# Softmax attention, soft mixture of experts and a gated layer: inverse roots from Ln and Exp, attention in double steps

## The chip, the core and the metric

The kernel runs on one core of one Trainium2 chip. The metric is device time in microseconds (us), the median of several executions. Five engines work side by side, each through its own instructions in order: TensorE (PE in the profile, with its weight loads as PEld), VectorE (DVE), ScalarE (ACT), GpSimd (POOL) and SyncE (SP), which here only issues DMA transfers.

## What is computed

Three layers follow one another: attention over 4 batches x 12 heads (448 tokens, 64 columns a head), a soft mixture of experts, and a gated layer. The part that the change touches is the first:

```python
def rmsnorm(x, g):
    rms = np.sqrt(np.mean(x * x, axis=-1, keepdims=True) + 1e-06)
    return x / rms * g
q_n, k_n = (rmsnorm(q, g_q), rmsnorm(k, g_k))
scale = 1.0 / np.sqrt(q.shape[-1])
scores = scale * np.matmul(q_n, k_n.transpose(0, 1, 3, 2))
scores = scores - np.max(scores, axis=-1, keepdims=True)
attn = np.exp(scores)
attn = attn / (np.sum(attn, axis=-1, keepdims=True) + 1e-09)
return np.matmul(attn, v).astype(np.float32)
```

Its output is the `x` of `_moe_ref` (logits, two softmaxes, 8 experts with relu), and that one's output is the input of `(x @ w_a) * (x @ w_b) @ w_out`.

## The kernel before

**Attention.** Heads are worked on in 24 pairs. The loop `for j in range(NPAIR + 1)` (L597) has one turn for a pair, and eight steps `s8` in it; a step is one block of 112 query rows of one head, numbered `n = 8 * j + s8`. What a step issues on each engine stands in the order of the code, since PE, ACT, POOL and SP follow the order of the program in this part; only DVE's order is chosen by a scheduler when the kernel is built.

A block goes through these functions. `score(n)` (L346) makes 112 x 448 scores with two matmuls (L357, L358; tile `pss`, one bank of PSUM, pool `ps_s` with three) and DVE searches the row maxima (L359, `nmx`). `expo(n)` (L363) takes the exponential on ACT (L368, tile `p`) and sums it. `ptrans(n)` (L374) transposes `p` with four PE instructions (L381, tile `pspt`, pool `ps_p` with two banks) and copies the result to `pt` on ACT (L387), or on DVE (L385) in two of eight steps. `av` (L389) multiplies the transposed probabilities of the pair before with `v` (L395, tile `psv`). In the loop, step n issues `score(n + 2)`, `expo(n + 1)`, in odd steps `av`, and `ptrans(n)`.

**The queries and keys to come.** The pairs ahead are made ready in the same loop. POOL squares (`square`, L252, tile `sq`, two buffers), DVE sums (`sumsq`, L260), and `rsqrt(p)` (L271) computes the inverse root on DVE alone: a bit trick gives a first guess, and three Newton steps follow, 12 small instructions of 112 x 16 elements in all (L281 to L291), which `tick` spreads between other work. `normalise(p)` (L294) multiplies on POOL. `emit_T(p, 0)` and `emit_T(p, 1)` (L310) transpose queries and keys (L324, tile `pst`), ACT writes a rounded part to the tile `e` (L326, L329) and DVE the rest (L327, L330). `e` has one buffer. `emit_Z(p)` (L335) then issues six DMA transfers on SP (L342 to L344, three for each head) that rearrange `e` into the tiles `z` which `score` reads; there are four, two for a pair. So the ACT write to `e` for the next pair waits until all six transfers of this pair have landed. In turn j, `emit_T(j + 2, 0)` stands in step 4, `emit_T(j + 2, 1)` in step 5, `emit_Z(j + 2)` in step 6, and the first `score` that reads these tiles in step 6 of turn j + 1.

**Other work in the loop.** `bcast` (L417; tile `psbc`, ACT copy `rd` L426) and `finish` (L429) divide the attention output. From turn 7 on, parts of the mixture of experts' first stage (`moe_tasks`, L443) are put in, one `task()` in each of the steps 3, 6 and 7. `pst`, `psbc` and the tasks take PSUM banks from the pool `ps_m` (two).

**Prologue.** Before the loop, pairs 0 to 3 are prepared (L555 to L589) and the first scores issued; `warm` issues matmuls that compute nothing needed.

**After attention.** The experts run on weights that SP streams from memory (L136), into seven places that take over attention's memory and a ring of five; then the gated layer. Neither is edited.

## Time and profile before

| | us |
|---|---|
| median of 3 runs | 597.33 (596.6 to 600.82) |
| profiled execution | 597.8, of which the span from first to last instruction is 596.0 |
| attention loop, first `score` to last `finish` | about 19.5 to 349.6 |
| busy: PE, DVE, ACT, POOL | 561.1, 388.2, 354.5, 116.5 |
| mean granted TensorE clock | 0.990 |

Busy time is what the profile gives each instruction from start to end; PE's instructions overlap in it. The chain of waits is a better guide to what sets the end: it is followed back from the last instruction, at each point to whatever was waited for, and gives each piece only the time that it adds. "issue" in it is a short hand-over.

### The profile page before, as it was taken

How to read it: one execution, taken by the hardware profiler on the slowest of the kernel's cores; microseconds unless marked ns; L12 is line 12 of the kernel's file. 1: busy time of each engine (PE TensorE's matmuls, PEld its weight loads, DVE VectorE, ACT ScalarE, POOL GpSimd, SP SyncE). 2: the span in 40 equal slices, each digit the busy share in tenths (PEclk: the TensorE clock that was granted, in tenths of full speed). 3: DMA queues.
4: the chain of work that ended last, by engine and by line, in shares of the span. 5: the costliest groups of instructions: out<-in, count | busy, mean ns of one | idle time of the engine just before them, and what ended most of it. 6: DMA issues, size and time to landing. Idle time of an engine off the chain costs nothing.

```text
span 596.0 us, 11201 instructions
## 1 busy us (share of the span) xinstructions
PE 561.1 (94%) x4008; PEld 369.1 (62%) x4008; DVE 388.2 (65%) x919; ACT 354.5 (59%) x797; POOL 116.5 (20%) x135
## 2 busy tenths in 40 slices
PE   6889899999999999999999998898999999999997
PEld 6655555555655565655656545443585656589996
DVE  6888898888899888898776621122227988742210
ACT  4667777778787777877778721111168989542210
POOL 2234343333343343333110000010100000300000
PEclk9999999999999999999999999989999999999999
DMA  5965677786777978696766789999999994002332
GB/s 145 224 164 139 158 175 173 208 230 196 190 221 170 251 177 244 146 268 167 219 184 154 273 343 340 426 408 423 425 425 419 382 398 186 1 27 80 87 95 84
DMA packets 39575, 134.52 MB, mean 226 GB/s; under 512 B 5856, under 2 KB 25312, under 8 KB 33120
## 3 DMA queue, kind: packets, MB, share of 16 engines
q1 hardware_dynamic: 39520, 133.81, 71.2%
q8 instruction: 32, 0.52, 0.4%
q14 instruction: 23, 0.19, 0.1%
HBM read 95.26 MB, written 5.51 MB: 169 GB/s over the span
## 4 chain that ended last, share of the span: by engine, by line
PE 65%; DVE 11%; DMA 10%; ACT 6%; SPq 5%; issue 3%; POOL 0%; ACTq 0%; DVEq 0%
PE psv L395 9%; PE pspt L381 9%; DMA z<-e 7%; PE pss L357 4%; PE pss L358 4%; PE psM L936 4%; PE psh L695 4%; PE pso L1136 3%; PE psS L719 3%; PE pso L1137 3%; PE pso L1138 3%; SPq L343 2%; PE pst L324 2%; DVE nmx L359 2%; PE psL L183 2%
## 5 line engine op out<-in xcount | busy, mean ns | idle before, releaser
L368 ACT ACTIVATE p<-pss,nmx 112x448 f32<-112x448 f32 x192 | 123.4, 643 | 26.0 <-DVE nmx L359 13.5
L359 DVE TENSOR_REDUCE nmx<-pss 112x1 f32<-112x448 f32 x192 | 117.7, 617 | 19.7 <-PE pss L358 18.2
L381 PEld LDWEIGHTS pspt<-ident,p 112*112 112x112 f32 x768 | 80.4, 133 | 78.1 <-ACT pt L387 32.4
L381 PE MATMUL pspt<-ident,p 112*112 112x112 f32 x768 | 110.0, 266 | 1.1 <-ACT p L368 0.9
L395 PE MATMUL psv<-pt,v 112*64 112x448 f32 x368 | 90.3, 569 | 1.0 <-DVE xT L436 1.0
L387 ACT COPY pt<-pspt 112x448 f32<-112x448 f32 x144 | 76.8, 533 | 21.4 <-PE pspt L381 20.5
L357 PE MATMUL pss<-z 128*112 128x448 f32 x192 | 85.2, 444 | 1.7 <-DMA z<-e 1.6
L300 POOL TENSOR_TENSOR n<-xw,rinv 112x512 f32<-112x512 f32 x46 | 48.1, 1066 | 173.6 <-PE pst L324 140.1
L358 PE MATMUL pss<-z 128*112 128x448 f32 x192 | 70.5, 367 | 0.0
L252 POOL TENSOR_TENSOR sq<-xw 112x512 f32<-112x512 f32 x40 | 40.9, 1041 | 0.6 <-DMA xw<-in_q_dram 0.4
L1155 DVE COPY ot<-pso 128x384 f32<-128x384 f32 (+1 forms) x14 | 7.6, 543 | 49.5 <-PE pso L1140 49.5
L357 PEld LDWEIGHTS pss<-z 128*112 128x112 f32 x192 | 34.0, 177 | 9.0 <-issue 7.4
L368 ACT ACTIVATION_READ_ACCUMULATOR p<-pss,nmx 112x1 f32 x192 | 39.4, 205 | 0.0
L816 DVE SCALAR_TENSOR_TENSOR xw<-wu_w,top 128x768 int32<-128x768 int32 x24 | 22.3, 956 | 25.5 <-ACT top L802 25.5
L1136 PE MATMUL pso<-Mh,t 128*128 128x384 f32 x112 | 37.9, 338 | 0.5 <-DVE Ml L965 0.5
L1137 PE MATMUL pso<-Ml,t 128*128 128x384 f32 x112 | 37.7, 337 | 0.0
L1138 PE MATMUL pso<-Mh,t 128*128 128x384 f32 x112 | 37.7, 337 | 0.0
L324 PE MATMUL pst<-ident,n 112*128 112x112 f32 x192 | 27.4, 268 | 10.6 <-ACT rd L426 7.1
L395 PEld LDWEIGHTS psv<-pt,v 112*64 112x64 f32 x368 | 18.3, 135 | 30.7 <-issue 22.5
L385 DVE COPY pt<-pspt 112x448 f32<-112x448 f32 x48 | 29.7, 619 | 10.4 <-PE pspt L381 9.5
L358 PEld LDWEIGHTS pss<-z 128*112 128x112 f32 x192 | 34.2, 178 | 0.7 <-issue 0.6
L260 DVE TENSOR_REDUCE ssq<-sq 112x8 f32<-112x512 f32 x48 | 32.1, 675 | 2.8 <-ACT sq L250 2.6
(177 smaller groups left out, 938.1 us busy)
## 6 DMA issues: line engine op xcount, KB each, us to landing
wu_w<-in_moe_w_dram SPq DMA_DIRECT2D x38, 1536.0 KB, 10.8
z<-e SPq DMA_DIRECT2D x48, 336.0 KB, 4.6
z<-e SPq DMA_DIRECT2D x48, 224.0 KB, 4.4
r<-in_moe_w_dram SPq DMA_DIRECT2D x7, 1536.0 KB, 8.3
xw<-in_moe_w_dram SPq DMA_DIRECT2D x4, 1536.0 KB, 13.4
xw<-in_q_dram SPq DMA_DIRECT2D x24, 224.0 KB, 4.3
xw<-in_k_dram SPq DMA_DIRECT2D x24, 224.0 KB, 4.1
z<-e SPq DMA_DIRECT2D x48, 112.0 KB, 4.4
```

The costliest lines, as they stand in the source:

```text
L252: pool.tensor_tensor(out=sq, in0=a, in1=a, op=ALU.mult)
L300: (eng if eng and i == 0 else pool).tensor_tensor(out=n_t[p][:, i].rearrange("p c h d -> p h c d"), in0=qk_t[p][:, i].rearrange("p h (c d) ...
L357: pe.matmul(ps, x, z[:, 1, :], start=True, stop=False)
L358: pe.matmul(ps, x, z[:, 2, :], start=False, stop=True)
L359: dve.tensor_reduce(out=nm_of[n // 8][:, h % 2, c:c + 1], in_=ps, axis=AX.X, op=ALU.max, negate=True)
L368: act.activation(out=t, in_=ps_of.pop(n), func=AF.Exp, bias=nm_of[n // 8][:, h % 2, c:c + 1], accum_out=den_t[n // 8][:, h % 2, c:c + 1],)
L381: pe.transpose(ps[:, kc * P:(kc + 1) * P], src[:, kc * P:(kc + 1) * P], ident[0:P, 0:P])
L387: act.copy(out=o, in_=i)
L395: pe.matmul(av_t[p][hd * D:(hd + 1) * D, 0:S], v_t[p][hd][:, kc, :], pt_t[2 * p + hd][:, kc, :], start=(kc == 0), stop=(kc == NC - 1),)
L1136: pe.matmul(o, ch[:, m], Mh[:, m, c], start=(m == 0), stop=False)
L1137: pe.matmul(o, ch[:, m], Ml[:, m, c], start=False, stop=False)
L1138: pe.matmul(o, cl[:, m], Mh[:, m, c], start=False, stop=False)
```

## The change

Three things change together.

1. `rsqrt(p)` takes its first guess from ACT: `Ln` of the sum of squares and `Exp` of minus half of that, and one Newton step of three DVE instructions follows. It is called in step 0 of turn j for pair j + 3, instead of step 7 for pair j + 4. A table of ACT's functions is loaded by hand at the start.
2. The eight steps of a turn become four double steps `s4`. `score(n)` now makes two blocks of scores in a tile of two banks, and one DVE search gives both maxima. A double step issues `expo(n + 2)`, `ptrans(n)`, `expo(n + 3)`, `ptrans(n + 1)`, then `score(n + 4)` (both blocks), then `av`. `emit_T(j + 2, 0)` stands at the end of `s4 == 2`, `emit_T(j + 2, 1)` and `emit_Z(j + 2)` at the end of `s4 == 3`, with two tasks behind them.
3. Buffers: `ps_s` has two tiles of two banks, `ps_p` is gone and its tiles come from `ps_m`, which has three banks; `p` has three buffers, `sq` one.

```diff
-        sqp = c1.enter_context(tc.tile_pool(name="sqp", bufs=2))
+        sqp = c1.enter_context(tc.tile_pool(name="sqp", bufs=1))
-        pp = c1.enter_context(tc.tile_pool(name="pp", bufs=2))
+        pp = c1.enter_context(tc.tile_pool(name="pp", bufs=3))
-        ps_s = c1.enter_context(tc.tile_pool(name="ps_s", bufs=3, space=PSUM))
-        ps_p = c1.enter_context(tc.tile_pool(name="ps_p", bufs=2, space=PSUM))
+        ps_s = c1.enter_context(tc.tile_pool(name="ps_s", bufs=2, space=PSUM))
-        ps_m = c1.enter_context(tc.tile_pool(name="ps_m", bufs=2, space=PSUM))
+        ps_m = c1.enter_context(tc.tile_pool(name="ps_m", bufs=3, space=PSUM))
...
-            mf = ssq_t.pop(p).rearrange("p a c -> p (a c)")
...
-            for _ in range(3):
-                small.append((p, lambda: dve.tensor_tensor(out=t, in0=yf, in1=yf, op=ALU.mult)))
...
+            x = ssq_t.pop(p).rearrange("p a c -> p (a c)")
+            act.activation(out=t, in_=x, func=AF.Ln, bias=ssq_eps[0:P])
+            act.activation(out=yf, in_=t, func=AF.Exp, scale=-0.5)
+            small.append((p, lambda: dve.scalar_tensor_tensor(
+                out=t, in0=yf, scalar=-0.5, in1=yf, op0=ALU.mult, op1=ALU.mult)))
+            small.append((p, lambda: dve.scalar_tensor_tensor(
+                out=t, in0=x, scalar=D * 1e-6, in1=t, op0=ALU.add, op1=ALU.mult)))
+            small.append((p, lambda: dve.scalar_tensor_tensor(
+                out=yf, in0=t, scalar=1.5, in1=yf, op0=ALU.add, op1=ALU.mult)))
...
+            ps = ps_s.tile([128, 2, 512], F32, tag="s", name="pss")[0:P, :, 0:S]
+            for i in range(2):
+                x = z[:, 0, (c + i) * P:(c + i + 1) * P]
+                pe.matmul(ps[:, i], x, z[:, 1, :], start=True, stop=False)
+                pe.matmul(ps[:, i], x, z[:, 2, :], start=False, stop=True)
+                ps_of[n + i] = ps[:, i]
+            dve.tensor_reduce(out=nm_of[n // 8][:, h % 2, c:c + 2], in_=ps, axis=AX.X, op=ALU.max, negate=True)
...
-            ps = ps_p.tile([P, 512], F32, tag="pt", name="pspt")[:, 0:S]
+            ps = ps_m.tile([128, 512], F32, tag="m", name="pspt")[0:P, 0:S]
...
+                for i in range(2):
+                    expo(n + 2 + i)
+                    if live:
+                        ptrans(n + i)
+                score(n + 4)
+                av(j - 1, s4)
+                if s4 == 0:
+                    if j > 0:
+                        rsqrt(j + 3)
+                    spread(j - 1)
+                    square(j + 4, 0)
+                elif s4 == 1:
+                    sumsq(j + 4, 0)
+                    square(j + 4, 1)
+                elif s4 == 2:
+                    bcast(j - 1)
+                    normalise(j + 3)
+                    emit_T(j + 2, 0)
+                    if j == 0:
+                        emit_T(j + 2, 1)
+                        emit_Z(j + 2)
+                else:
+                    if j > 0:
+                        emit_T(j + 2, 1)
+                        emit_Z(j + 2)
+                    load_v(j + 1)
+                    sumsq(j + 4, 1)
+                for _ in range(1 + (s4 == 3)):
+                    if s4 in (1, 3) or (s4 == 0 and j > NPAIR - HP):
+                        task()
```

How the rows of the programs move is shown at three places. The first is PE in the second half of turn 1, before: `psbc` and the transposes `pst` stand between single scores, and the second group of `pst` (the keys of pair 3) is followed by five more groups before the turn ends.

```order
L381 MATMUL pspt<-ident,p_549 112x112 x4
L324 MATMUL pst<-ident,n_415 128x112 x4
L422 MATMUL psbc<-ident,bc 128x112 x4
L357 MATMUL pss<-z_142 112x448
L358 MATMUL pss<-z_142 112x448
L395 MATMUL psv<-pt_355,v_177 64x448
L395 MATMUL psv<-pt_408,v_177 64x448
L381 MATMUL pspt<-ident,p_565 112x112 x4
L324 MATMUL pst<-ident,n_415 128x112 x4
L357 MATMUL pss<-z_139 112x448
L358 MATMUL pss<-z_139 112x448
L381 MATMUL pspt<-ident,p_596 112x112 x4
```

The same place after the change, from `psbc` to the second group of `pst`:

```order
L422 MATMUL psbc<-ident,bc 128x112 x4
L323 MATMUL pst<-ident,n_402 128x112 x4
L381 MATMUL pspt<-ident,p_521 112x112 x4
L381 MATMUL pspt<-ident,p_530 112x112 x4
L357 MATMUL pss<-z_138 112x448
L358 MATMUL pss<-z_138 112x448
L357 MATMUL pss<-z_138 112x448
L358 MATMUL pss<-z_138 112x448
L395 MATMUL psv<-pt_355,v_177 64x448
L395 MATMUL psv<-pt_408,v_177 64x448
L323 MATMUL pst<-ident,n_402 128x112 x4
L381 MATMUL pspt<-ident,p_566 112x112 x4
```

What moved: the two groups of `pst` are now a whole double step apart, the second is the last thing of the turn, and the next pair's tile (`z_138`) is already read at this point of turn 1, where before it was read after the second `pst`.

The second place is ACT between the two writes to `e` (`L326` and `L329` before, `L325` and `L328` after), before (turn 2):

```order
L326 ACTIVATE e_574<-pst 128x448
L426 COPY rd<-psbc 128x448
L368 ACTIVATE p_596,den<-pss,nmx 112x448
L329 ACTIVATE e_574<-pst,few 128x448
L368 ACTIVATE p_621,den<-pss,nmx 112x448
```

and after (turn 2):

```order
L426 COPY rd<-psbc 128x448
L325 ACTIVATE e_715<-pst 128x448
L368 ACTIVATE p_723,den<-pss,nmx 112x448
L387 COPY pt_680<-pspt 112x4x112
L368 ACTIVATE p_731,den<-pss,nmx 112x448
L387 COPY pt_680<-pspt 112x4x112
L328 ACTIVATE e_715<-pst,few 128x448
```

What moved: two exponentials and two copies now lie between the two writes, where one copy and one exponential lay before.

The third place is DVE at the end of the prologue, at the first search for maxima (L359 before, L360 after). Before:

```order
L281 TENSOR_SCALAR ssq_316<-ssq_316 112x16
L288 TENSOR_TENSOR nt<-rinv_297 112x16
L283 TENSOR_SCALAR rinv_321<-ssq_316 112x16
L289 SCALAR_TENSOR_TENSOR nt<-nt,ssq_255 112x16
L285 TENSOR_SCALAR rinv_321<-rinv_321 112x16
L359 TENSOR_REDUCE nmx<-pss 112x1
L291 SCALAR_TENSOR_TENSOR rinv_297<-nt,rinv_297 112x16
L288 TENSOR_TENSOR nt<-rinv_321 112x16
L359 TENSOR_REDUCE nmx<-pss 112x1 x2
```

and after (`rinv_282` and `rinv_299` are the roots of pairs 2 and 3, as `rinv_297` and `rinv_321` before):

```order
L329 SCALAR_TENSOR_TENSOR e_245<-pst,few,e_245 128x448
L286 SCALAR_TENSOR_TENSOR nt<-rinv_282 112x16
L288 SCALAR_TENSOR_TENSOR nt<-ssq_240,nt 112x16
L261 TENSOR_REDUCE ssq_294<-sq 112x8
L290 SCALAR_TENSOR_TENSOR rinv_282<-nt,rinv_282 112x16
L261 TENSOR_REDUCE ssq_294<-sq 112x8
L286 SCALAR_TENSOR_TENSOR nt<-rinv_299 112x16
L288 SCALAR_TENSOR_TENSOR nt<-ssq_294,nt 112x16
L290 SCALAR_TENSOR_TENSOR rinv_299<-nt,rinv_299 112x16
L360 TENSOR_REDUCE nmx<-pss 112x2
```

What moved: the first search stood in the middle of the Newton steps of pairs 2 and 3, and now stands behind all of them.

## Rows read from the trace of the kernel before

**Rows 1.** Windows: length, busy us (instructions) by engine, granted clock, DMA share, GB/s

```profile
119.00:313.80 194.80, 188.88 (x1244) 114.90 (x1245) 166.08 (x422) 147.76 (x386) 61.27 (x66) 1.00 0.78 206
...
349.00:490.00 141.00, 130.15 (x1264) 77.96 (x1265) 58.56 (x111) 60.41 (x83) 7.57 (x15) 0.99 0.98 400
```

**Rows 2.** Chain of waits near 210 us: start, us added, engine, tile, line

```profile
209.48 0.53 PE pspt L381 x4
210.01 0.20 PE pss L357
...
210.42 0.38 PE pspt L381 x4
...
211.21 0.90 PE psv L395 x4
...
213.77 0.38 PE pst L324 x4
```

**Rows 3.** Chain of waits, 89 to 106 us: SP's issues and the landing

```profile
89.83 3.97 DMA z<-e
...
97.36 0.47 SPq L342
...
98.52 1.07 SPq L344
...
101.40 4.42 DMA z<-e
```

**Rows 4.** Timeline of ACT: the copy `rd`, one in each turn, turns 1, 7, 21

```profile
42.58 0.53 ACT L426 COPY rd<-psbc 128x448 f32<-128x448 f32 x1
...
118.97 0.55 ACT L426 COPY rd<-psbc 128x448 f32<-128x448 f32 x1
...
313.81 0.56 ACT L426 COPY rd<-psbc 128x448 f32<-128x448 f32 x1
```

**Rows 5.** Timeline of the prologue: start, us, engine, line, operation

```profile
7.70 0.15 DVE L561 SCALAR_TENSOR_TENSOR few<-few 128x1 f32<-128x1 f32 x1
...
15.17 0.63 ACT L329 ACTIVATE e<-pst,few 128x448 fp32r<-128x448 f32 x1 [0.20 <-PE pst L324]
...
20.86 0.63 ACT L368 ACTIVATE p<-pss,nmx 112x448 f32<-112x448 f32 x1 [4.02 <-DVE nmx L359]
```

**Rows 6.** Chain of waits, 24 to 60 us

```profile
33.54 0.43 ACT pt L387
...
34.01 0.73 ACT p L368 x2
...
45.49 1.69 PE psv L395 x4
...
50.03 0.54 PE pspt L381 x4
```

**Rows 7.** Groups by line: busy us, mean ns of one, idle before

```profile
L359 DVE TENSOR_REDUCE nmx<-pss 112x1 f32<-112x448 f32 x192 | 117.7, 617 | 19.7 <-PE pss L358 18.2
L330 DVE SCALAR_TENSOR_TENSOR e<-pst,few,e 128x448 fp32r<-128x448 f32 x24 | 16.1, 671 | 0.1
L326 ACT ACTIVATE e<-pst 128x448 fp32r<-128x448 f32 x24 | 13.2, 550 | 20.9 <-DMA z<-e 13.9 <-PE pst L324 4.9 <-PE pss L358 2.0
L474 ACT ACTIVATE nm<-nm 128x1 f32<-128x1 f32 x2 | 0.6, 294 | 3.5 <-DVE nm L473 3.5
L100 ACT ACT_TABLE_LOAD x1 | 1.3, 1283 | 0.7 <-PEq L1204 0.7
```

**Rows 8.** Timeline near 204 us: POOL's multiplication and two Newton instructions

```profile
201.13 0.17 DVE L289 SCALAR_TENSOR_TENSOR nt<-nt,ssq 112x16 f32<-112x16 f32 x1
...
204.06 2.04 POOL L300 TENSOR_TENSOR n<-xw,rinv 112x512 f32<-112x512 f32 x2 [7.72 <-PE pst L324]
204.11 1.01 DVE L289 SCALAR_TENSOR_TENSOR nt<-nt,ssq 112x16 f32<-112x16 f32 x1
```

**Rows 9.** Chain of waits, 110 to 140 us: a late landing

```profile
127.84 5.77 DMA z<-e
```

87 lines of the change are left out of this document (26 added, 61 removed).

## The prediction

> **What bounds the kernel now.** I read the windows first. In the stretch of attention from turn 7 on, PE is busy 188.9 of 194.8 us; behind attention the DMA engines are busy 98% of the time [rows 1]. So the later stages follow attention's end and move with it as a block; the question is what attention does. The chain of waits tells it: near 210 us it is PE alone. Two steps cost 0.53 us (first group of `pspt`, behind `psv`) + 0.38 (second group) + 4 x 0.205 (scores) + 0.90 (`av`) = 2.63 us [rows 2]. Four of these and three groups of transposes (two `pst`, one `psbc`) at 0.38 make 11.7 us a turn as PE's own floor. The copies `rd` mark the turns: from turn 1 to 7 six turns take 76.4 us, 12.73 each, and from 7 to 21 fourteen take 194.8, 13.92 each [rows 4]. In the first stretch nearly nothing but the 11.7 is to be done, so 1.0 us a turn is stall. In the second, the tasks add PE work: 188.9 / 14 = 13.5 a turn bounds the floor from above, since the busy times of PE overlap a little; I take 13.35, so about 0.55 a turn is stall.
>
> The stall of the first stretch is a loop that the chain shows whole: the six transfers have landed at 89.83 + 3.97 = 93.80, ACT writes `e`, PE transposes the keys, DVE writes its part, SP issues six times, and the next six have landed at 101.40 + 4.42 = 105.82 [rows 3]: 12.02 us, against PE's 11.7. A late landing (5.77 us [rows 9] for 4.42) adds 1.35.
>
> **The change part by part.** *PE's work* is the same: the groups are reordered, and the dear first `pspt` behind `psv` still comes once in a double step. 11.7 stays.
>
> *Fewer DVE instructions.* Nine Newton instructions and three before them go, three stay; two searches become one. DVE is not on the chain where PE is, so this pays nothing by itself; it only lets DVE's part of `e` come sooner. The size: a Newton instruction takes 0.17 us alone and 1.01 when POOL's 2.04 us multiplication runs [rows 8]. One search takes 0.617 [rows 7]; a search of two blocks is not in the trace, and lies between 0.62 (nothing for the second) and 1.23 (no saving); I take 1.1, nearest to twice the row. It hides either way: its exponentials come a double step later.
>
> The row of 1.01 us fits a rule of the Trainium skill (SBUF, section Who interferes with whom): a DVE instruction with two SBUF inputs and a GpSimd instruction that reads SBUF use one read interface, and the second to start waits for the whole of the other. By the rule the three new instructions, which have two such inputs, still wait behind POOL, up to 2 us a turn; by the row alone I would charge 0.8 each time. In the new order they stand behind DVE's part of `e`, so neither enters the sum.
>
> *Ln and Exp.* Not in the trace; the nearest ACT instructions on few columns take 0.294 us [rows 7]. I take 0.3 each, 0 to 0.6 as bounds for both when they overlap others. ACT then has 8 x 0.73 + 6 x 0.43 [rows 6] + 0.55 [rows 7] + 0.63 [rows 5] + 0.45 + 0.6 = 10.7 us a turn, under PE's 11.7: hidden, but only 1 us is left.
>
> *The z loop.* This is the term that speaks against the change. Between ACT's two writes to `e` there were one copy and one exponential; now there are two exponentials and two copies: 2 x (0.73 + 0.43) = 2.32 us. The loop becomes 0.55 (`e`, queries) + 2.32 + 0.63 (`e`, keys) + 0.67 (DVE's part [rows 7]) + 101.40 - 97.36 = 4.04 (first to sixth issue) + 4.42 (landing) [rows 3] + some 0.1 of hand-over = 12.75. That is 0.7 longer than 12.02. Against it stands a DVE that is less late. So a turn without tasks takes 12.75 at best; with one landing in five late by 1.35, 13.0.
>
> *When scores read z.* Before, a whole turn lay between the issue and the first score; now `emit_Z` is last in a turn and `score` of that tile stands in `s4 == 2` of the next. From the last `pst` to that score PE has 2 x 2.63 + 0.91 = 6.2 us of work. The first head's tile needs 0.63 + 0.67 + (98.52 - 97.36 = 1.16, third issue) + 4.42 + 0.1 = 7.0. PE waits 0.8 in a turn without tasks; this lies inside the 12.75 to 13.0 (11.7 + 0.8 = 12.5). With tasks, 1 us and more of their work stands behind the last `pst`, and the wait is covered.
>
> *Three banks for everything.* Behind the last `pst` come two tasks, then `pspt`: the third in turn gets the bank of `pst`, which DVE frees 0.63 + 0.67 = 1.3 us after PE's end. Two `psx` tasks last 0.7, so PE loses 0 to 0.6 in the eleven or so turns with tasks. I take 0.3 on average, 0.2 over fourteen turns.
>
> *Prologue.* Roots of pair 0: DVE waits for `gg` until 7.70 [rows 5]; then three instructions of 0.17 instead of the rest of two Newton chains, so `e` and the first transfers come about 1.6 us sooner. But ACT now issues Ln of pair 2 behind its second write to `e` of pair 1 (15.17 + 0.63 [rows 5], some 0.8 later by my count, so 16.6), and behind that follow in series, with one `sq` buffer: two pairs of Ln and Exp (1.2), two squares (1.25), two sums (1.35), Newton (0.5): 21.0, then the first search. The first exponential starts at 22.1 instead of 20.86 [rows 5]. From there to the end of turn 1 ACT has 18 exponentials, 12 copies, two pairs of writes to `e`, one `rd`, Ln and Exp: 13.1 + 5.2 + 2.4 + 0.5 + 0.6 = 21.8 us; nothing in that stretch waits longer for `z`, since pair 2's roots no longer wait behind searches. So turn 1 ends at about 44.7, with 0.8 us of scores done ahead of where they stood. Before, it ended at 50.03 + 0.54 = 50.57, having waited and then run `psv` at 1.69 us where it takes 0.90 [rows 6, 2]. Gain 5.9 + 0.8 = 6.7, between 2 and 8.
>
> **Sum**, against the profiled 597.8: prologue -6.7; turns 1 to 7: 6 x (13.0 - 12.73) = +1.6; turns 7 to 21: 12 turns with tasks at PE's floor, two without at 13.0 instead of 11.7 (+2.6), the banks (+2.8): 14 x 13.35 + 2.6 + 2.8 = 192.3 instead of 194.8, -2.5; the rest 0. That is -7.6: 590.2, rounded to 590.0. The median of the runs shown is 597.33, 0.5 below the profiled one.
>
> **Rivals.**
> *All stalls go* (chance 0.16). If a DVE that is less busy lets `e` come early and landings are quick, PE sets every turn: -6.7 - 6 x 1.0 - 14 x 0.55 = -20.4: 577. For it: the chain near 210 us is PE alone. Against: the loop of 12.75 is longer than 11.7.
> *The z loop sets every turn* (0.14). If landings take 5.77 as a rule, or ACT reaches the second write to `e` one exponential late, the loop is 14.1 to 14.2 in both stretches: 6 x 1.45 + 14 x 0.25 - 6.7 = +5.5: 603. From 14.2 on, it ends over 1% slower. For it: issue and first use are 5 us closer together. Against: 4.42 is the commoner landing.
> *The gain is given back* (0.23). The prologue gains 3 only, and the banks cost the full 0.6 in eleven turns, so that turns 7 to 21 take 186.9 + 2.6 + 6.6 = 196.1: -3 + 1.6 + 1.3 = about 598.
> *Table loads* (0.02). If Ln and Exp did not sit in one loaded table with the rest, two loads of 1.283 us [rows 7] a turn would put ACT at 13.3 against 11.7: 20 x 1.3 = +26, 617. The new program has one load in all, as before. The Trainium skill (ScalarE: Activation LUTs, section Table sets: the hidden batching unit) says that one set holds both; no run here has shown it yet.
>
> **How the numbers follow.** The forecast has 0.45, with 585 to 595 as its own range. About 1% is what a measurement of this kernel can tell from no change: faster is under 591.4, slower over 603.3. Faster: three quarters of 0.45, all of 0.16 and a little of the third rival, 0.52. Slower: most of 0.14 and the 0.02, 0.14. The rest, 0.34, is within 1%. The range from 577 to 603 leaves out half of the first rival, half of the second and the last.
>
> **What would show it.** Right: `rd` in turn 1 at about 41 instead of 42.58, turns of 12.7 to 13.2 up to turn 7, the six landings still in the chain there, small waits of `pss` for `z`, and one table load. Wrong: turns over 13.5 in the first stretch (the loop was underrated), turns at 11.7 (it was overrated), a first exponential before 20 or after 24 us, PE's clock under full speed in the loop, or a later stage that changes its length.

## The result and the profile after

The changed kernel takes **603.63 us** (median of 4 runs, 601.82 to 608.16) against 597.81 for the kernel before, run beside it (4 runs): ratio **1.0105**, 95% interval 1.0071 to 1.014. It is slower by 1%, where 590.0 was forecast, and 603 was the upper end of the range. The profiled execution took 601.82 us, its span 600.0, against 597.8 and 596.0 before.

First three windows of the changed kernel, cut at its `rd` of turns 1, 7 and 21 and where the experts' transfers set the pace (columns as in [rows 1]), then these three `rd` in the timeline of ACT.

```profile
45.60:125.00 79.40, 73.50 (x471) 44.65 (x470) 57.74 (x95) 59.22 (x164) 27.82 (x30) 1.00 0.65 156
125.00:322.40 197.40, 189.48 (x1244) 116.33 (x1242) 142.58 (x259) 148.32 (x411) 60.96 (x66) 1.00 0.76 205
...
356.00:494.00 138.00, 127.75 (x1264) 77.29 (x1263) 57.75 (x110) 60.44 (x83) 7.58 (x15) 1.00 1.00 416
```

```profile
45.62 0.53 ACT L426 COPY rd<-psbc 128x448 f32<-128x448 f32 x1 [0.89 <-PE psbc L422]
...
124.95 0.53 ACT L426 COPY rd<-psbc 128x448 f32<-128x448 f32 x1 [0.93 <-PE psbc L422]
...
322.40 0.53 ACT L426 COPY rd<-psbc 128x448 f32<-128x448 f32 x1 [0.86 <-PE psbc L422]
```

Beside [rows 4]: turns 1 to 7 take 79.33 us, where they took 76.39; turns 7 to 21 take 197.45, where they took 194.84. That is 2.9 and 2.6 us more, and PE is busy 189.48 of 197.40 us in the second stretch, where it was busy 188.88 of 194.80 [rows 1]. Behind turn 21 the account goes up and down again: the last `finish` starts 5.5 us later than before (354.5 for 349.0), the experts' first matmul (`psh`) 6.1 (366.8 for 360.7), their last `psh` 4.1 (431.2 for 427.1), and the end comes 4.0 later. So the experts give 2.0 us back; in the stretch bound by transfers the DMA share is 1.00 for 0.98. (`rd` itself now stands two blocks later in a turn's order, so 45.62 for 42.58 is no loss by itself: the last `av` of turn 1 starts at 47.63 and ends at 48.53, where it ended at 50.03 before, at the start of the group behind it [rows 6].)

Two groups of lines answer to [rows 7]: the search of two blocks, and the one table load.

```profile
L360 DVE TENSOR_REDUCE nmx<-pss 112x2 f32<-112x896 f32 x96 | 104.5, 1089 | 35.4 <-PE pss L358 34.5
...
L92 ACT ACT_TABLE_LOAD x1 | 1.3, 1283 | 0.7 <-PEq L1208 0.7
```

In the chain of waits of the changed kernel a turn without tasks (start, us added, what) looks like this; beside [rows 2, 3]:

```profile
82.83 0.43 PE pss L357
...
88.24 0.55 PE pst L323 x4
88.81 0.64 ACT e L328
89.48 0.69 DVE e L329
90.19 0.47 SPq L341
90.71 0.59 SPq L342
91.35 4.15 DMA z<-e
95.64 0.43 PE pss L357
```

and the waits of PE for `z` in turns 1 to 7 (total us, times, longest):

```profile
PE pss L357 <- DMA z<-e: 3.8, 3, 2.1
```

From score to score it is 95.64 - 82.83 = 12.81 us. PE works from 82.83 to 88.79; then the chain leaves it, for 6.85 us: keys copied, three transfers issued, landed, and the score that waited for `z` can start. PE has other work in that time but for 0.8 us at its end (0.85 ahead of the score at 82.83). Behind such a stand the first score adds 0.43 us to the chain, where the scores that follow add 0.20.

### The profile page after: what moved, and what is told of

Same layout as the page of the kernel before. It is cut to its first block, busy times and chain, and to the rows that moved or that the text cites. A ratio compares the mean times of both kernels' runs of the same rounds, so it can differ in the third digit from the quotient of the medians.

```text
span 600.0 us, 10699 instructions
## 1 busy us (share of the span) xinstructions
PE 559.2 (93%) x4008; PEld 372.7 (62%) x4008; DVE 348.6 (58%) x607; ACT 357.2 (60%) x845; POOL 113.5 (19%) x136
## 4 chain that ended last, share of the span: by engine, by line
PE 76%; ACT 7%; DMA 6%; DVE 5%; issue 2%; SPq 1%; POOL 0%; ACTq 0%; DVEq 0%; POOLq 0%
PE psv L395 13%; PE pspt L381 12%; PE pss L357 6%; PE pss L358 6%; PE psM L940 4%; PE pst L323 3%; PE pso L1140 3%; PE psS L723 3%; PE pso L1141 3%; PE pso L1142 3%; PE psh L699 3%; DMA z<-e 3%; PE psbc L422 2%; PE psL L185 2%; DMA wu_w<-in_moe_w_dram 2%
## 5 line engine op out<-in xcount | busy, mean ns | idle before, releaser
L360 DVE TENSOR_REDUCE nmx<-pss 112x2 f32<-112x896 f32 x96 | 104.5, 1089 | 35.4 <-PE pss L358 34.5
L381 PE MATMUL pspt<-ident,p 112*112 112x112 f32 x768 | 95.1, 265 | 10.1 <-ACT p L368 3.8
L381 PEld LDWEIGHTS pspt<-ident,p 112*112 112x112 f32 x768 | 76.0, 134 | 41.3 <-ACT p L368 14.8
L357 PE MATMUL pss<-z 128*112 128x448 f32 x192 | 77.2, 402 | 6.2 <-DMA z<-e 3.8
L358 PE MATMUL pss<-z 128*112 128x448 f32 x192 | 70.6, 368 | 0.0
L253 POOL TENSOR_TENSOR sq<-xw 112x512 f32<-112x512 f32 x40 | 41.6, 1040 | 50.6 <-DVE ssq L261 43.9
L357 PEld LDWEIGHTS pss<-z 128*112 128x112 f32 x192 | 34.0, 177 | 10.2 <-DVE pt L385 5.0
L940 PE MATMUL psM<-w,G 128*128 128x512 f32 x64 | 33.6, 607 | 0.3 <-DVE w L820 0.3
## 6 DMA issues: line engine op xcount, KB each, us to landing
xw<-in_moe_w_dram SPq DMA_DIRECT2D x4, 1536.0 KB, 12.2
```

Source lines behind the costliest of these rows:

```text
L357: pe.matmul(ps[:, i], x, z[:, 1, :], start=True, stop=False)
L358: pe.matmul(ps[:, i], x, z[:, 2, :], start=False, stop=True)
L360: dve.tensor_reduce(out=nm_of[n // 8][:, h % 2, c:c + 2], in_=ps, axis=AX.X, op=ALU.max, negate=True)
L381: pe.transpose(ps[:, kc * P:(kc + 1) * P], src[:, kc * P:(kc + 1) * P], ident[0:P, 0:P])
L940: pe.matmul(o, G[:, r], W[:, c], start=st, stop=sp_)
```

## The experiments

Each kernel was run beside the kernel before; the ratio is to that, with its 95% interval. The turns are us per turn, from the starts of `rd` in the profiled execution.

| kernel | ratio | turns 1-7 | 7-16 | 16-21 |
|---|---|---|---|---|
| before | 1 | 12.73 | 13.91 | 13.93 |
| changed | 1.0105 (1.0071-1.014) | 13.22 | 13.89 | 14.48 |
| u1_roots | 0.989 (0.9839-0.994) | 12.42 | 13.63 | 13.76 |
| u2_steps | 1.0382 (1.0314-1.0451) | 14.68 | 14.58 | 15.18 |
| t1_tasks | 1.0053 (1.0015-1.0091) | 12.95 | 14.11 | 14.06 |
| t2_zearly | 1.0069 (1.0032-1.0106) | 12.71 | 14.15 | 15.13 |
| t3_prologue | 1.0034 (1.0003-1.0065) | 12.88 | 13.90 | 14.80 |
| t4_all | 0.9981 (0.9947-1.0015) | 12.77 | 14.04 | 14.12 |
| u3_banks | 1.0251 (1.0187-1.0314) | 13.50 | 14.88 | 15.43 |
| u4_banks_z | 1.0085 (1.0048-1.0123) | 12.47 | 14.51 | 14.93 |
| v1_zlate | 1.0132 (1.0095-1.017) | 12.95 | 14.86 | 14.92 |
| v2_pool | 0.9895 (0.988-0.991) | 12.57 | 13.59 | 13.71 |
| v3_first | 0.9952 (0.9925-0.998) | 12.58 | 13.63 | 13.89 |
| v4_tight | 0.994 (0.9914-0.9966) | 12.03 | 13.74 | 13.89 |
| w1_step_sooner | 1.0277 (1.0243-1.031) | 13.48 | 14.59 | 15.64 |
| w2_sooner_prol | 1.0269 (1.0229-1.0309) | 13.55 | 14.82 | 15.22 |
| w3_tight_early | 0.9838 (0.9807-0.9868) | 12.23 | 13.62 | 13.86 |
| x1_two_e | 1.005 (1.002-1.008) | 13.06 | 13.79 | 14.80 |
| x2_two_e_sooner | 1.0013 (0.9987-1.0039) | 12.02 | 13.90 | 15.23 |
| x3_two_e_single | 0.9794 (0.9751-0.9838) | 12.05 | 13.42 | 13.87 |

### The two halves of the change apart

`u1_roots` takes only the roots, `u2_steps` only the double steps:

```diff
 # u1_roots, against the kernel before
-            small.append((p, lambda: dve.tensor_scalar(
-                out=mf, in0=mf, scalar1=1.0 / D, scalar2=1e-6, op0=ALU.mult, op1=ALU.add)))
...
+            act.activation(out=t, in_=x, func=AF.Ln, bias=ssq_eps[0:P])
+            act.activation(out=yf, in_=t, func=AF.Exp, scale=-0.5)
 # u2_steps, against the changed kernel: the same lines the other way round
```

> The kernel before with the roots by Ln and Exp alone; attention in single steps, two score banks, four banks for the rest, as before. Theory (the double steps carry the loss, the roots are about neutral): the loop of z and the tasks run as before, so turns 1 to 7 take 12.7 and turns 7 to 21 take 13.9; pair 0's roots are done 1.6 us sooner, of which the first turns keep 0 to 3: 594 to 598. Rival (the roots carry the loss, because Ln and Exp stand between the exponentials and because the sum of pair 4 now comes up sooner on DVE's queue): a search of turn 0 stands behind that sum, turn 1 ends 1 to 3 us later than before, and the time is 600 or more.

> The changed kernel with the old twelve Newton instructions for the roots; the double steps, two-bank score tiles and the new place of the z loop stay. Theory (the double steps carry the loss): turns 7 to 21 take 14.0 to 14.2, turns 1 to 7 13.0 to 13.4, since nothing there hung on the roots, and the time is 602 to 608, like the changed kernel or a little over it because DVE has nine more instructions a turn between the searches. Rival (the roots carry it): about 597.

The roots alone gain 1.1% (592.36 us), the double steps alone lose 3.8% (621.51 us): the theory that the steps carry the loss holds. Two things were not expected. In single steps the roots pay 0.2 to 0.3 us a turn on average, and nothing up to the end of turn 1, whose last `av` ends at 50.78 us, 0.75 later than before. And the halves don't add up: with double steps the same roots are worth 3.8 - 1.05 = 2.8%. The chain of waits of `u2_steps` shows why:

```profile
92.94 0.55 ACT e L326
93.52 0.62 DVE e L327
...
94.43 1.01 DVE nmx L361
...
96.06 0.86 DVE rinv L291
96.94 0.97 DVE nt L288
97.91 0.61 DVE e L330
98.53 0.47 SPq L342
...
102.55 4.43 DMA z<-e
...
107.08 0.55 ACT e L326
```

This is a loop over `e`, 107.08 - 92.94 = 14.14 us long: queries, keys, issue, landing, and the next queries, which must not overwrite `e` before its transfers have landed. PE is not in the chain there. From the start of DVE's first part of `e` to that of its second (93.52 and 97.91) are 4.4 us, most of it DVE's own queue: a search, and Newton instructions, two of which take 0.86 and 0.97 us.

The same instructions are dear in the prologue of `u1_roots`, in the timeline of POOL and DVE (start, us, engine and line, operation):

```profile
19.07 2.04 POOL L300 TENSOR_TENSOR n<-xw,rinv 112x512 f32<-112x512 f32 x2 [5.09 <-DVE rinv L291]
...
20.12 1.03 DVE L287 SCALAR_TENSOR_TENSOR nt<-rinv 112x16 f32<-112x16 f32 x1 [0.68 <-ACT rinv L286]
21.09 1.04 POOL L254 TENSOR_TENSOR sq<-xw 112x512 f32<-112x512 f32 x1
21.18 0.98 DVE L289 SCALAR_TENSOR_TENSOR nt<-ssq,nt 112x16 f32<-112x16 f32 x1
22.19 0.17 DVE L291 SCALAR_TENSOR_TENSOR rinv<-nt,rinv 112x16 f32<-112x16 f32 x1
```

Beside POOL's three instructions, which end at 22.13 us, two of three DVE instructions take about 1 us; alone, the third takes 0.17. With this agrees what the Trainium skill (SBUF, section Who interferes with whom) says of DVE instructions with two SBUF inputs and GpSimd.

### The first turn

`t3_prologue` is the changed kernel with pair 4's squares and sums at the end of turn 0, and its root a double step later:

```diff
-                    square(j + 4, 0)
+                    if j > 0:
+                        square(j + 4, 0)
...
                     normalise(j + 3)
+                    if j == 0:
+                        square(j + 4, 0)
```

> The changed kernel, with the squares and sums of pair 4 moved in turn 0 from the first double steps to the last, and the root of pair 4 one double step later in turn 1. Theory 'prologue': DVE's second search for maxima stands behind a sum that waits for the load of pair 4 (landed at 23.8 us), so exponentials stop from 23.3 to 26.8 us; without that wait the second search starts at about 22.1 us and the kernel is 3 to 5 us faster (about 599). The other theories: the loop's first turns wait for z anyway and give back all but 1 us.

The reason for it, in the timeline of the changed kernel:

```profile
22.13 0.63 ACT L368 ACTIVATE p<-pss,nmx 112x448 f32<-112x448 f32 x1 [1.81 <-DVE nmx L360]
...
23.96 1.04 POOL L253 TENSOR_TENSOR sq<-xw 112x512 f32<-112x512 f32 x1 [3.31 <-DMA xw<-in_q_dram]
...
25.03 0.69 DVE L261 TENSOR_REDUCE ssq<-sq 112x8 f32<-112x512 f32 x1 [2.94 <-POOL sq L253]
25.63 1.08 DVE L360 TENSOR_REDUCE nmx<-pss 112x2 f32<-112x896 f32 x1
...
26.75 0.63 ACT L368 ACTIVATE p<-pss,nmx 112x448 f32<-112x448 f32 x1 [3.28 <-DVE nmx L360]
```

The first exponential comes at 22.13 us, as forecast (22.1). But on DVE's queue the sum for pair 4 stands ahead of the second search; it waits 2.94 us for a square whose input has not landed, and ACT then 3.28 us for the search. Without that the kernel took 600.45 us, 0.7% less than the changed one (the quotient of the two ratios is 0.993). By the profiles `rd` of turn 1 is 1.5 us sooner on average: 43.80, 45.40 and 45.71 in the three kernels with this edit, 45.55 to 47.70 in six without. So this is a part of the loss, but only a part; and where another wait stands ahead of it (`w2_sooner_prol`, below) the same edit gives nothing.

### Tasks

`t1_tasks` puts one task behind three of the four double steps, instead of one behind the second and two behind the last:

```diff
-                for _ in range(1 + (s4 == 3)):
-                    if s4 in (1, 3) or (s4 == 0 and j > NPAIR - HP):
-                        task()
+                if s4 in (0, 1, 3) or j > NPAIR - HP:
+                    task()
```

> The changed kernel, with one task at the end of the double steps 0, 1 and 3 instead of one behind step 1 and two behind step 3. Theory 'tasks in pairs': behind the last transposes of the keys stand two tasks and then pspt, which wants the PSUM bank that ACT and DVE still hold, and the second task of a pair often waits for the first one's copy; PE loses 0.7 to 1.2 us in some eleven turns there, so this kernel is 6 to 10 us under the changed one (about 595). Theory 'z late': the waits of scores for the transfers of z cost the time; then nothing comes back (602 to 604), or it grows by 2, since the tasks covered the wait. Theory 'prologue': no change.

602.29 us, a ratio 0.5% under the changed kernel's with intervals that overlap, and turns 7 to 21 in 197.30 us, as before the edit (197.45): no gain there. The turns with a transposed `x` and its sum got shorter (13.3 and 13.0 for 13.7 and 14.9), the one with the task `lrep` longer (17.6 for 14.6). The waits moved: in the turn of 17.6 us PE stands 2.0 us for copies of `pt` and for `e`, and that explains only a part of its length.

### Banks

`u3_banks` gives the double steps back tiles of one bank: three for scores, four for the rest, two searches. `v2_pool` does the opposite edit on the better half: single steps with `u1_roots`' roots, and the changed kernel's banks, four for scores and three shared by the rest.

```diff
 # u3_banks, against the changed kernel
-        ps_s = c1.enter_context(tc.tile_pool(name="ps_s", bufs=2, space=PSUM))
+        ps_s = c1.enter_context(tc.tile_pool(name="ps_s", bufs=3, space=PSUM))
...
-        ps_m = c1.enter_context(tc.tile_pool(name="ps_m", bufs=3, space=PSUM))
+        ps_m = c1.enter_context(tc.tile_pool(name="ps_m", bufs=4, space=PSUM))
 # v2_pool, against u1_roots
-        ps_s = c1.enter_context(tc.tile_pool(name="ps_s", bufs=3, space=PSUM))
-        ps_p = c1.enter_context(tc.tile_pool(name="ps_p", bufs=2, space=PSUM))
+        ps_s = c1.enter_context(tc.tile_pool(name="ps_s", bufs=4, space=PSUM))
...
-        ps_m = c1.enter_context(tc.tile_pool(name="ps_m", bufs=2, space=PSUM))
+        ps_m = c1.enter_context(tc.tile_pool(name="ps_m", bufs=3, space=PSUM))
```

> The changed kernel with scores in tiles of one bank again: three banks for scores (instead of two tiles of two banks), four for everything else (instead of three), and two searches a double step. Theory (the missing fourth bank makes the transposes of e^s wait behind the last tile of turned keys): the waits of `pspt` for ACT's and DVE's parts of `e` in the turns with tasks go, turns 7 to 21 fall from 14.1 to 13.8 or less, and the time to 598 to 601. Rival (tasks that need each other's copies, and the z loop, make the stall; the banks only show it): turns 7 to 21 stay at 14.0 to 14.2 and the time at 602 to 605.

> The kernel before with the roots by Ln and Exp (single steps, z loop in its old place), and with the banks cut as the double steps cut them: four for scores, three for all the rest together, where there were three for scores, two for the transposes of exponentials and two for the rest. Theory (sharing three banks costs in the turns with tasks, where transposes come behind tiles and tasks that have not been copied out): turns 7 to 21 go from 13.7 to 13.9 or more with waits of `pspt` for copies of tasks and `e`, turns 1 to 7 stay: 595 to 600. Rival (the place of the z loop alone costs): 591 to 594, no such waits.

`v2_pool` took 593.05 us, the same as `u1_roots`, with the same turns: sharing three banks costs nothing by itself, and the theory of the banks fell there. `u3_banks` tells nothing for it either: it took 614.06 us, because scores that run four ahead now lack a bank, as its waits of PE say (total us, times, longest):

```profile
PE pss L357 <- ACT p L368: 10.7, 22, 1.9
```

### The place of the z loop

`t2_zearly` moves the keys' tile and the transfers of z in all turns to the end of the third double step, where the queries' tile already stands; `u4_banks_z` is that edit on `u3_banks`; `t4_all` is `t1_tasks`, `t2_zearly` and `t3_prologue` together.

```diff
                     emit_T(j + 2, 0)
-                    if j == 0:
-                        emit_T(j + 2, 1)
-                        emit_Z(j + 2)
+                    emit_T(j + 2, 1)
+                    emit_Z(j + 2)
```

> The changed kernel, with the second group of transposes of a pair and its transfers issued at the end of double step 2 in every turn, as turn 0 does, instead of at the end of double step 3. Theory 'z late': scores wait for z about 1.1 us in each of the six turns before tasks begin and 1.5 in the two later ones without tasks; a double step more of room takes all of that away, 7 to 10 us (about 595), and the turns 1 to 7 fall from 13.2 to about 12. Theory 'tasks in pairs': 0 to 3 us from the bank of the transposes, which is no longer the one wanted behind the tasks. Theory 'prologue': no change.

> The same with one-bank score tiles and four banks for the rest, and with the last tile of turned keys and the six transfers of z issued at the end of the third double step of every turn, not the fourth. Theory (issuing early gains nothing with three banks because the transposes then run out of banks): with four banks turns 1 to 7 fall under 12.4 and turns 7 to 21 to 13.7 or less, so the time is 590 to 596. Rival (what is saved at z comes back because `e` waits for loads, or because the tasks' order sets the turn): within 2 us of the kernel with four banks alone.

> The three edits together. If the three causes are apart from one another, the gains add: 603.6 less 8, 8 and 4 is about 584, under both kernels. If one cause covers the others, the sum stays at the largest of them, about 594.

None of the hoped-for gains came. `t2_zearly` took 604.07 us: its early turns are 12.4 to 12.5 us where landings are quick, but two tiles of turned pairs and the broadcast one behind the other fill the three banks, and the transposes wait instead (waits of PE's weight loads in turns 1 to 21; PE itself stands 10.2 us for it):

```profile
PEld pspt L381 <- DVE e L326: 14.6, 20, 0.7
```

In `u4_banks_z` the extra bank takes that wait away: 603.2 for 614.06 us, and early turns of 12.17 us. `t4_all` took 598.47 us, the same as the kernel before. In its profile it is 3.5 us ahead of the changed kernel at `rd` of turn 21, of which 2.7 come from turns 1 to 7 (76.59 for 79.33 us) and 0.2 from what lies ahead of them.

`v1_zlate` puts the z loop of the single steps where the double steps put it: one edit on `u1_roots`, which moves no bank, no task and no search.

```diff
-        TA, TB, TZ = 4, 5, 6
+        TA, TB, TZ = 5, 7, 7
```

> The kernel before with the roots by Ln and Exp (single steps, banks as before), and with one more edit: the two tiles of turned pairs come behind steps 5 and 7 of a turn and the six transfers of z behind step 7, where the double steps put them, instead of 4, 5 and 6. Theory (the place of the z loop is what the double steps cost in the early turns): turns 1 to 7 go from 12.4 to 12.9 or more, turns 7 to 21 from 13.7 to 13.9 or more, together at least 5 us: 597 to 603. Rival (the three shared banks are what costs, the place alone is covered): turns as without this edit, 591 to 594.

608.15 us instead of 592.36, a ratio 2.4% above that of `u1_roots`. The whole of the double steps loses 2.2% against `u1_roots`, but the two losses don't lie in the same turns. In the early turns the edit costs about what the theory says, 12.80 for 12.38 us over the first five, yet a turn 1 that ends 4.8 us sooner still covers it: the last `av` of turn 6 ends at 109.77 us, in `u1_roots` at 111.11. All of the loss comes behind it, and there the edit does one thing more than the double steps do. In every second turn from turn 6 to 18, SP issues a load of the experts' weights behind step 6, so it now comes ahead of the six transfers; in the changed kernel and in `u1_roots` it comes behind them. The timeline of SP's queue, and of ACT, in `v1_zlate`:

```profile
104.48 0.45 SPq L138 DMA_DIRECT2D wu_w<-in_moe_w_dram  x1
...
113.86 1.15 SPq L344 DMA_DIRECT2D z<-e  x1
...
224.15 0.54 ACT L326 ACTIVATE e<-pst 128x448 fp32r<-128x448 f32 x1 [2.44 <-DMA z<-e]
```

The first of the six, issued at 109.39, is 9.54 us in the chain of waits; the slowest of the run lands after 10.3 us, against 7.8 in the changed kernel. ACT's write to `e` waits for such landings, the exponentials stand behind it, and `pspt` waited 15 times for exponentials (12.2 us in all). In the changed kernel ACT never waits for a landing in turns 7 to 21. So this run bears on the place in the early turns alone.

`w1_step_sooner` tries the obvious cure on the changed kernel: everything of the z loop one double step sooner, one tile a double step. `w2_sooner_prol` adds `t3_prologue`'s edit.

```diff
+                    if j > 0:
+                        emit_T(j + 2, 0)
                 elif s4 == 2:
...
-                    emit_T(j + 2, 0)
-                    if j == 0:
-                        emit_T(j + 2, 1)
-                        emit_Z(j + 2)
+                    if j == 0:
+                        emit_T(j + 2, 0)
+                    emit_T(j + 2, 1)
+                    emit_Z(j + 2)
```

> The changed kernel with the z loop one double step sooner and still one tile of turned pairs a double step: queries behind the second double step of a turn, keys and the six transfers of z behind the third (instead of third and fourth; turn 0 as it was). Theory (the place of the z loop is what the double steps lose): turns 1 to 7 fall from 13.2 to 12.0 to 12.4, and turns 7 to 21 from 14.1 to 13.7 to 13.9 with no wait of scores for z: 592 to 597. Rival (in the turns with tasks it is the order of the tasks, with waits for their own copies): turns 1 to 7 fall as much but turns 7 to 21 stay at 14.0 to 14.2: 597 to 600.

> The same with pair 4's squares, sums and roots a double step or two later in turn 0, as in the run on the prologue. Theory (the sum of pair 4, ahead of the second search, costs the first turn 2 to 3 us): 2 to 4 us under the kernel without this edit, 589 to 594 if the place of the z loop is the cause. Rival (with z sooner the first turns wait for the transfers, and the sum is covered): the same within 1 us.

It is much slower, 614.9 us, against theory and rival; with the prologue's edit 614.38, the same within 1 us, as that rival said. The timeline of ACT and of SP's queue in `w1_step_sooner` tells why:

```profile
84.61 0.55 ACT L325 ACTIVATE e<-pst 128x448 fp32r<-128x448 f32 x1 [1.23 <-DMA z<-e]
...
87.56 0.64 ACT L328 ACTIVATE e<-pst,few 128x448 fp32r<-128x448 f32 x1
...
93.02 1.83 SPq L343 DMA_DIRECT2D z<-e  x1
...
98.84 0.54 ACT L325 ACTIVATE e<-pst 128x448 fp32r<-128x448 f32 x1 [3.74 <-DMA z<-e]
```

The scores no longer wait for z. Now the next queries do: ACT comes to them at 95.1 us and stands for 3.74 us until the last transfer, issued at 93.02, has landed 5.72 us later, since there is one `e`. The loop is 98.84 - 84.61 = 14.23 us here, of which 2.95 lie between queries and keys, one double step; the landing is a late one, and the turns up to turn 6 take 12.52 to 13.80 us.

### A second place for `e`

If that is so, a second `e` must cure it. `extra`, a buffer that holds nothing until turn 18, takes the odd pairs up to 17:

```diff
+                elif p % 2 == 1 and p < 18:
+                    e_t[p] = extra.bitcast(F32R)[:, 0:4 * S].rearrange("p (x s) -> p x s", s=S)
                 else:
                     e_t[p] = ep.tile([128, 4, S], F32R, tag="e", name=f"e{p}")
```

`x1_two_e` is the changed kernel with it, `x2_two_e_sooner` is `w1_step_sooner` with it.

> The changed kernel with a second place for `e`: odd pairs up to 17 are written into a buffer that lies idle until turn 18, so that in turns 1 to 16 the queries of one pair need not wait until the six transfers of the pair before have landed. Theory (with one `e` the path from queries to keys to issue to landing and back to the next queries is a loop, and the double steps make it longer than PE's work): turns 1 to 7 fall from 13.2 to 12.5 to 12.8 each, where scores wait for z, and turns 7 to 16 from 13.9 to 13.6 or less: 595 to 600. Rival (the scores' wait for z alone, or the tasks' order, sets the turns): turns as before within 0.1, 602 to 605.

> The changed kernel with the z loop one double step sooner (614.9 with one `e`) and with the second place for `e` up to pair 17. Theory (one `e` made that kernel slow: its queries stood a double step ahead of its keys and held ACT's queue until the landing): turns 1 to 7 fall from 13.5 to 11.7 to 12.2, turns 7 to 16 from 14.3 to 13.5 to 13.9: 588 to 598. Rival (banks: the transposes wait for DVE's part of `e` and for the tasks' copies, however many `e` there are): turns 1 to 7 at 12.2 to 12.8, turns 7 to 16 stay at 14 or more: 600 to 608.

`x2_two_e_sooner` takes 598.93 us, 2.6% less than `w1_step_sooner`. Its windows of turns 1 to 7 and 7 to 16:

```profile
45.55:117.69 72.14, 72.14 (x471) 44.42 (x470) 59.29 (x97) 58.99 (x164) 27.83 (x30) 1.00 0.75 186
117.69:242.75 125.06, 121.17 (x794) 74.36 (x793) 95.43 (x169) 95.37 (x266) 41.83 (x45) 1.00 0.78 205
```

In the first, PE is busy 72.14 of 72.14 us, in five turns of 11.72 to 11.75 us, the forecast's floor of 11.7, and a sixth of 13.49 that holds the first task. So the early turns are settled. They are set by two conditions, both longer than PE's work, and each hides the other: with the second `e` alone (`x1_two_e`, 601.38 us, its interval overlapping the changed kernel's) the early turns stay at 12.8 where landings are quick, because scores still wait for z, 4.4 us in turns 1 to 7; with the sooner place alone (`w1_step_sooner`) `e` is waited for; with both, neither is.

In turns 7 to 16, with tasks, nothing of the kind shows. They take 13.89 us in the changed kernel, and 13.79 and 13.90 with the second `e`, while single steps with the same roots take 13.4 to 13.7 (but for `v1_zlate`). What PE waits for there in `x2_two_e_sooner` (turns 7 to 21):

```profile
PE pspt L383 <- ACT xtok L516: 3.4, 8, 1.4
PE pset L491 <- ACT l L478: 1.9, 1, 1.9
PE pspt L383 <- DVE xtok L514: 1.1, 2, 0.5
```

Transposes wait for the copies of tasks ahead of them. Banks alone did not bring this (`v2_pool`), nor did the order of tasks alone (`t1_tasks`). That it takes both banks and double steps, in which two transposes follow a task with no score between, fits these lines; no run here isolates it, and it stays open.

### Single steps made better

`v3_first` puts the first scores of `u1_roots` ahead of pair 3's preparation and pair 4's squares behind step 5. `v4_tight` adds both tiles and the transfers behind step 5 in every turn. `w3_tight_early` does this on `u1_roots` in turns 1 to 6 alone. `x3_two_e_single` adds the second `e` to it.

```diff
 # v3_first, against u1_roots
+        score(0)
+        score(1)
+        expo(0)
         prep(3)
         norm(3)
...
 # v4_tight, against v3_first
-        TA, TB, TZ = 4, 5, 6
+        TA, TB, TZ = 5, 5, 5
 # w3_tight_early, against u1_roots
-                ts = (TA, TB, TZ) if j > 0 else (T0A, T0B, T0Z)
+                ts = (T0A, T0B, T0Z) if j == 0 else (5, 5, 5) if j <= HP else (TA, TB, TZ)
```

> The kernel before with the roots by Ln and Exp, and with the first two scores and the first exponential ahead of pair 3's squares, sums and roots, and pair 4's squares and sums behind the sixth step of turn 0 instead of the second. Theory (in the first turn DVE's queue, not PE or the transfers, holds the searches: with the roots alone the first search stands behind pair 3's two instructions of 1.04 and 0.99 us): first exponential at 19 to 21 us instead of 22.9, and the time falls by 1 to 3 us to 589 to 591. Rival (the first turns wait for z of pair 1 or for the loads of pair 3 anyway): the exponential comes sooner but turn 1 ends at the same time, 592.

> The same with both tiles of turned pairs and the transfers of z behind step 5 of a turn, instead of steps 4, 5 and 6: the loop over `e` gets one step (1.3 us) shorter. Theory (late landings are what is left over PE's floor in the early turns, 12.4 against 11.9): turns 1 to 7 take 11.9 to 12.1 each and the time is 1 to 4 us under that of the kernel without this edit. Rival (the two tiles one behind the other and the broadcast before them want the same two banks): PE waits for ACT's and DVE's parts of `e` in each turn, and the time is 2 us or more over it.

> The kernel before with the roots by Ln and Exp, and in turns 1 to 6 alone both tiles of turned pairs and the transfers of z behind step 5. Theory (the loop over `e` is what is left over PE's floor in the early turns, and the place behind step 5 harms only where tasks use the same two banks): turns 1 to 7 take 11.7 to 12.1 instead of 12.4 each, turns 7 to 21 stay at 13.6 to 13.7, so the time is 1 to 4 us under that of the roots alone: 588 to 592. Rival (what is gained early is waited for later): 592 to 594.

> The kernel before with the roots by Ln and Exp and with the tight place of the z loop in turns 1 to 6 (588.5), and with the second place for `e` up to pair 17. Theory (what is left over PE's floor in turns 7 to 16 of the single steps is the same loop): turns 7 to 16 fall from 13.6 to 13.4 or less, the time to 585.5 to 587.5. Rival (single steps have no such wait left in the turns with tasks): 588 to 589.

`v3_first` went the wrong way: 596.09 us, 3.7 more than `u1_roots`, and the first exponential at 22.99 us, no sooner (22.94 in `u1_roots`, where DVE did hold the first search). Its chain of waits shows what holds the first score once DVE is out of the way:

```profile
16.29 5.60 PE warm L185 x30
21.89 0.20 PE pss L357
...
22.99 0.72 ACT p L368 x2
```

Thirty warming matmuls stand ahead of it on PE. The preparation of pair 3, moved behind it, now stands between the exponentials (ACT waits 1.35 us there), and so does the sum of pair 4 in its later place: at 39.49 us ACT has waited 2.92 us for it. `v4_tight` brings the early turns to 11.7 us (12.03 on average, with one of 12.14 and a sixth of 13.32 that holds the first task) and lengthens those with tasks by 0.1. `w3_tight_early` keeps the one and drops the other: **588.52 us**. Most of its gain comes ahead of the early turns, though: the last `av` of turn 1 ends 3.5 us sooner than in `u1_roots`, where ACT had waited 2.8 us in turn 1 for the landing that frees `e`, and turns 1 to 7 give 1.1. With the second `e` it becomes **585.14 us**, ratio 0.9794 (0.9751 to 0.9838), the lowest of all, 3% under the changed kernel; the step from `w3_tight_early` lies within the two intervals. Its windows of turns 1 to 7 and 7 to 16:

```profile
39.31:111.61 72.30, 72.30 (x473) 43.51 (x472) 62.31 (x121) 60.59 (x165) 27.95 (x30) 1.00 0.77 187
111.61:232.41 120.80, 119.24 (x794) 73.10 (x795) 98.47 (x205) 97.32 (x267) 42.21 (x45) 1.00 0.84 219
```

PE is without a gap in the first and stands for 1.6 us of 120.8 in the second.

This kernel and `x2_two_e_sooner` have the same roots and the second `e`, and their turns 1 to 7 are alike (12.05 and 12.02). So what is left between them, 13.8 us or 2.2%, is a loss of the double steps that the place of the transfers in the early turns doesn't explain. By the profiles some 2 us of it lie ahead of the end of turn 1, some 4 in turns 7 to 16, and nearly 7 in 16 to 21, where the double steps of `x2_two_e_sooner` are back to one `e`.

## Why the prediction was wrong, step by step

Of the 11.6 us between the forecast and the profile (-7.6 and +4.0), the prologue is 5.2, turns 7 to 21 are 5.1 and turns 1 to 7 are 1.3.

**Prologue: -6.7 forecast, -1.5 measured.** The first exponential (22.13 us for 22.1), Ln (0.31 us) and Exp (0.22 us; 0.3 each taken), and the order up to the first search came as worked out. The step that failed is the one behind it: ACT's own 21.8 us up to the end of turn 1 were added up as if nothing held it, with a look at `z` alone ("nothing in that stretch waits longer for `z`"). From 22.13 to 48.53 us it took 26.4, and ACT waits 6.4 us of them for searches, the longest (3.28) behind the sum for pair 4, whose load had not landed: the next row of DVE's queue, behind those that were looked at. With that wait out of the way (`t3_prologue`) the kernel is 0.7% faster, some 4 us. The last `av` of turn 1 ended at 48.53 us, not 44.7 (22.1 and 21.8 make 43.9; the 0.8 up to 44.7 has no row). Two blocks of scores, 0.8 us, were done ahead by then, but the transposes of the keys (0.53) still stood behind it.

**Turns 7 to 21: -2.5 forecast, +2.6 measured.** Twelve turns were put at PE's floor of 13.35 because tasks would cover the wait for z. They do cover it: PE has no wait for z there, and a second `e` changes nothing in turns 7 to 16 (13.79 for 13.89 us). What failed is that PE then works at its floor. Of 197.40 us it is busy 189.48, where the sum had 14 x 13.35 = 186.9, and it stands 7.9, where the sum had 5.4. Most of the standing is for the tasks' own copies, which had no term; the three longest waits of PE in these turns are

```profile
PE pset L489 <- ACT l L476: 2.4, 1, 2.4
PE pspt L381 <- DVE e L329: 1.5, 2, 0.7
PE pspt L381 <- ACT xtok L514: 1.3, 3, 0.4
```

In all PE stands 0.5 us a turn in turns 7 to 16 of the changed kernel (0.4 with the second `e`) and 0.8 in turns 16 to 21. The floor itself is there to be had: where PE hardly waits (`x3_two_e_single`), it is busy 119.24 us in nine turns, 13.25 each. Why it is busy longer in the double steps, the runs don't show. The wait that the term for three banks named, `pspt` for DVE's part of `e`, came twice, 1.5 us of the 2.8 set down; it is no price of the banks alone, since `v2_pool` has the same banks and pays nothing.

**z loop: right in size, the wrong condition.** 13.0 was forecast for a turn without tasks on average, and the first five take 13.05, with one late landing in five (14.03) as taken. The sixth, 14.07 us, has a late landing as well, but also the first task, 1.63 us of PE's work (13.35 in `x1_two_e`); it makes 13.22 of the average of six, and +2.9 us of +1.6. For a quick landing 12.75 was forecast and 12.81 measured, but that is in part luck. The loop over `e` that gave 12.75 does not bind: a second `e` leaves these turns as they are. What binds is the scores' wait for z, and of this the sum was right about PE's stand (0.85 us for 0.8) and the latency behind the last `pst` (6.85 for 7.0), but made 12.5 of it; the first score behind the stand and the hand-over add the rest.

**Fewer DVE instructions: taken as nothing, worth 5 us in single steps.** The prediction said that this pays nothing by itself and only lets DVE's part of `e` come sooner, and gave that no number. But DVE's part of `e` is on the loop: `u1_roots` saves 1.9 us in turns 1 to 7 and 3.4 in 7 to 21 (191.42 for 194.84), with nothing else changed. In double steps it is worth some 17 us (2.8%). The argument "DVE is not on the chain where PE is" was taken from one place of the chain, near 210 us, where PE is alone [rows 2], although [rows 3] had shown another.

**The later stages** were to move as a block, with 0 in the sum; a later stage that changes its length was named as a sign of being wrong. One does: the last turns and the way to the experts add about 2 us, and the experts give 2.0 back. That these cancel is luck.

**The search of two blocks** took 1.089 us (1.1 taken), and **one table load** of 1283 ns was there, as before; the rule of the Trainium skill (ScalarE: Activation LUTs, section Table sets: the hidden batching unit), that Ln and Exp sit in one set, agrees with it.

**The rivals.** The time came out as in the second, 603 us, but by another way: the landing of z sets only the early turns. "The gain is given back" had the sign of the second stretch right (+1.3 for +2.6), with banks as its reason, which are not enough by themselves. The sum for *Table loads* has 20 x 1.3, where 13.3 against 11.7 makes 1.6 a turn; it bears on nothing, since there was one load. None of the rivals gave the gain of the roots to the loop. That the double steps lose is shown (`u2_steps`), and that in the early turns it is the place of the transfers that loses (`x2_two_e_sooner`); what loses in turns 7 to 21 is named by the waits but not isolated.

## What to carry to other kernels

Before a chain through several engines is moved by a step, write down both conditions that close it: when its result is read, and when its buffer may be written again. Here both were longer than PE's 11.7 us (12.8 for the reading, 12.5 to 13.8 for the writing once the reading was eased), so each edit that eased one ran into the other, and a second buffer with the sooner place took both away. And an instruction off PE's chain is not free if the chain that feeds PE passes through its queue: nine small DVE instructions were worth 1% in one layout and nearly 3% in another.

## What the runs showed of the hardware

A wait of PE can be paid twice. In `w1_step_sooner` PE had been busy without a gap (granted clock 1.00), then stood for 1.82 us for `e`, up to 73.23 us. In the window that holds the stand and the work behind it the granted clock is 0.72, with rows at the lower of its two levels (1.2 GHz; 0.50 from 75 to 77 us) beside rows at the higher (2.4 GHz):

```profile
60.20:71.00 10.80, 10.80 (x71) 6.59 (x69) 8.78 (x14) 7.58 (x23) 4.64 (x5) 1.00 0.67 154
71.00:77.20 6.20, 4.38 (x24) 3.65 (x20) 3.12 (x6) 5.16 (x14) 2.48 (x3) 0.72 0.25 71
```

Behind that wait a matmul of scores takes 0.37 us in the chain of waits (76.13 us), a turn later 0.20 (88.31 us). Not every wait does this: in the changed kernel PE stood 2.07 us for `z` up to 70.02 us, and the granted clock stays at 1.00 from 66 to 82 us. Which waits do, the runs don't show. In the first turns the clock goes with PE's work in the same way: from 24 to 39 us it is 0.89 in the changed kernel, where PE is busy 10.70 of 15.00 us, and 1.00 in `x3_two_e_single`, where it is busy 14.39 of 15.00.
